# A fused attention and feed-forward kernel: static PSUM tiles in place of pools, two score tiles ahead of the values, and copies issued one step later

## The chip, the core and the metric

The kernel runs on one core of a Trainium2 chip. TensorE (PE) multiplies and writes PSUM, VectorE (DVE) and ScalarE (ACT) read PSUM and work on SBUF, GpSimd (POOL) works on SBUF and issues the loads, SyncE (SP) issues stores and transposing transfers. The metric is the device time of one execution in microseconds (us). Each engine runs its instructions in order; semaphores order the engines among each other.

## What is computed

Attention with a cumulative decay over 8 batches of 8 heads (576 positions, head dimension 64), then a two-layer network over all 4608 positions:

```python
scores = q @ k.T / sqrt(D)
cum = cumsum(log(clip(f, 1e-4, 1)))
scores = where(causal, -1e9, scores + cum[i] - cum[j])
attn = softmax(scores)
x = (attn @ v), heads side by side       # 4608 x 512
h = x @ w_in                             # 512 x 2048
out = (h - tanh(h)) @ w_out              # 2048 x 512
```

Inputs and output are float32; the matmuls run on float16 operands.

## The kernel before

Attention is done in 32 *slots*, one for each batch and each pair of heads. A slot has seven *score tiles* (ti 0 to 6): a score tile is one or two matmuls of L384 (with some small ones for decay and mask in the first slots) into one PSUM bank, an exp by ACT from PSUM to SBUF (L399), and in slots from 5 on a causal mask by POOL (L413). After ti 1 of a slot come the *values* of the slot before: thirty matmuls of L423 into the `av` bank pair, then division by DVE (L429 to L431) to `xn`, then `turn`, which transposes `xn` into the ring `XR` (by PE in batch 0, by transposing DMA later).

The network is done in nine *units* of 512 positions. A unit has sixteen *mlp1 tiles*: four matmuls of L458 into one bank from `m_bank()`, tanh by ACT to `th` (L465), and `gt = mb + th` by DVE (L476; tanh is taken of the negative). Then come fourteen *product* steps (L512), eight matmuls each. They form the second layer by a scheme of seven block products: three running sums X, W and Y in PSUM, each read when a part of it is final. X is copied to SBUF as `part` by ACT (L519) after products 1, 6 and one more, and goes on accumulating in the same bank; `settle` adds a bank to such a part by DVE (L545, L542) or copies it out by ACT (L536), and stores it. For units from 1 on X lies in the bank of `ps_tr`, W and Y come from `m_bank()`.

The order of everything is written out by hand; no scheduler moves it. `first_slot` runs the first five slots by the lists in `FIRST` ("g" is a group of two score tiles, "s" one score tile, "va" and "vb" the values of the two heads, "x" and "y" a turn, "h" an mlp1 tile without its last matmul, "m" one network step). From slot 5 on `att_items` lists a slot's attention work, and the loop at the end deals network steps (`step()`, L587) between it: seven or eight a slot, five in slots 5 to 7, so that 30 steps of a unit take four slots. A score tile and a network step mostly alternate; in a slot with eight steps ti 0 and ti 1 stand together, in one with seven also ti 2 and ti 3. Units 7 and 8 are the tail: no scores are left there.

PSUM has eight banks. Two hold `av`, one is `ps_tr`. The other five change hands at slot 4: up to slot 3 they are one bank for transpositions (`ps_t2`) and two pairs for groups of scores (`ps_two`); from slot 4 on three for `m_bank()` (`ps_m`) and two for single score tiles (`ps_sc`). The pools hand out a new tile at each call, and the framework puts a semaphore wait in front of the first write to it, on the last reader of the tile that had this place before.

In slots 7 and 8, `trans` brings the next batch's Q and K from PSUM to SBUF by ACT ("AA") in place of DVE ("VV") for some calls.

Of the kernel before, what the change touches and what calls it, by code (L numbers as in the profile page):

```python
# [8 lines left out]
FP32 = mybir.dt.float32  # L9
FP16 = mybir.dt.float16  # L10
AF = mybir.ActivationFunctionType
# [12 lines left out]
def kernel(  # L24
# [10 lines left out]
    nc = tc.nc  # L35
    P = 128
# [6 lines left out]
    NPAIR = H // 2  # L43
# [6 lines left out]
    UW = 512  # L50
# [11 lines left out]
    PSUM = bass.MemoryType.PSUM  # L62
    ps_av = ctx.enter_context(tc.tile_pool(name="ps_av", bufs=1, space=PSUM))
    ps_tr = ctx.enter_context(tc.tile_pool(name="ps_tr", bufs=1, space=PSUM))
    POOLS = {}
    turn_of = [0]

    def m_bank():
        return POOLS["m"].tile([P, UW], FP32, tag="m", name="mb")

    win = wpl.tile([P, NCH, DFF], FP16)
    wout = wpl.tile([P, NFT, DM], FP16)
# [7 lines left out]
    qn, kn = ([t[0:S // NT6, :].rearrange("p (h n d) -> p h n d", h=H, n=NT6) for t in raw] for raw in (qraw, kraw))  # L80
# [218 lines left out]

    def t_bank():  # L300
        turn_of[0] += 1
        if "t" in POOLS and turn_of[0] % 2:
            return POOLS["t"].tile([P, UW], FP32, tag="t2", name="t32")
        return ps_tr.tile([P, UW], FP32, tag="tr", name="t32")

    def trans(b, c, src, dst, engs):
# [31 lines left out]
    LAST = 3  # L338
# [18 lines left out]

    def scores(b, c, tis, how):
        n2 = len(tis)
        if "t" in POOLS and tis[0] == LAST:  # L360
            banks = t_bank().rearrange("p (o w) -> p o w", o=1)
        else:
            banks = POOLS["s"].tile([P, 2 if "t" in POOLS else 1, UW], FP32, tag="sc", name="ps")
        if tis[0] == LAST:
            eb = EL[(b * NPAIR + c) % 3].rearrange("p (o w) -> p o w", o=1)
        else:
            g, o = PLACE[tis[0]]
            if b == 0:
                if o == 0:
                    EB[(b, c, g)] = gtp.tile([P, 2, UW], FP16, tag="gt", name="e2")  # L370
                eb = EB[(b, c, g)][:, o:o + n2, :]
            else:
                eb = aex.tile([P, 1, UW], FP16, tag="e", name="e")
        late = []
        for i, ti in enumerate(tis):
            ps, e = banks[:, i, :], eb[:, i, :]
            for a, j, i0, n, col in TILES[ti]:
                h = 2 * c + a
                while late and late[-1][2] is ps:
                    decay(*late.pop(0))  # L380
                edge = min(P, n) if how != "late" and i0 == j * P else 0
                direct = b == 0 and (h == 0 or h == 1 and ti in (4, 5))
                rows = D if direct and h else D + 3
                nc.tensor.matmul(out=ps[:, col:col + n], lhsT=KT[b % 2][0:rows, h, j * P:(j + 1) * P],  # L384
                                 rhs=QT[b % 2][0:rows, h, i0:i0 + n], start=True, stop=not (edge or direct))
                args = (b, h, ps, j, i0, n, col, edge, direct)
                if direct and len(tis) > 1:
                    late.append(args)
                else:
                    decay(*args)  # L390
                for ib in range(j, NJ):
                    w0 = min(ib * P, S - P)
                    if i0 <= ib * P < i0 + n:
                        E[(b, c, a, j, ib)] = e[:, col + w0 - i0:col + w0 - i0 + P]
        for args in late:
            decay(*args)
        lo = min(x[4] for x in TILES[tis[0]])
        hi = max(x[4] + x[3] for x in TILES[tis[0]])
        nc.scalar.activation(out=eb[:, :, lo:hi], in_=banks[:, 0:n2, lo:hi], func=AF.Exp, scale=qscale)  # L399
        if how != "late":  # L400
            return
        ti, e = tis[0], eb[:, 0, :]
        col, cp, step, wd = MASKS[ti]
        dims = [[step, cp, 0]] * (cp > 1)
        if b < FAR:
            dims = dims + [[D, wd // D, D]] * (wd > D) + [[D // 2, 2, 1], [1, D // 2, 2]]
        else:
            dims = dims + [[1, wd, 1]]
        parts = [(0, dims)] if len(dims) < 4 else [(o * step, dims[1:]) for o in range(cp)]
        for o, dims in parts:  # L410
            view = e[:, col + o:col + o + wd]
            view = bass.AP(view.tensor, view.offset, [list(view.ap[0])] + [[x, n] for x, n, _ in dims])
            nc.gpsimd.affine_select(out=view, in_=view, compare_op=ALU.is_ge, fill=0.0,  # L413
                                    base=0, pattern=[[y, n] for _, n, y in dims], channel_multiplier=-1)
# [65 lines left out]
    def sums(u, i, which):  # L480
# [5 lines left out]
        for n in which:  # L486
# [2 lines left out]
            eng = nc.gpsimd if (n < 3 and i < 2 or n == 2 and i == 2) and u > NU - 3 else nc.vector  # L489
            eng.tensor_tensor(out=dst, in0=x, in1=y, op=op)  # L490

    def product(u, n, g):
        t0 = g * P
        chain = (1, 6, 7, 4) if u == 0 else (1, 6, 5, 3)
        where = "X" if n in chain else "W" if n == 2 else "Y"
        last = u == NU - 1 and where == "Y"
        if last:
            where += str(g)
        first = n in (1, 2, 5 if u == 0 else 7)
        if first and (g == 0 or last):  # L500
            M2[(u, where)] = ps_tr.tile([P, DM], FP32, tag="tr", name="px") if where == "X" and u else m_bank()
        ps = M2[(u, where)]
        left = {1: lambda k: GT[(u, k)][:, t0:t0 + P],
                2: lambda k: GT[(u, K2 + k)][:, t0:t0 + P],
                3: lambda k: SUM[(u, k // 2)][:, 2, k % 2, t0:t0 + P],
                4: lambda k: GT[(u, K2 + k)][:, T2 + t0:T2 + t0 + P],
                5: lambda k: SUM[(u, k // 2)][:, 0, k % 2, t0:t0 + P],
                6: lambda k: SUM[(u, k // 2)][:, 1, k % 2, t0:t0 + P],
                7: lambda k: GT[(u, k)][:, T2 + t0:T2 + t0 + P]}[n]
        right = {1: B11, 2: B21, 3: B22, 4: WT4, 5: WT1, 6: WT2, 7: WT3}[n]  # L510
        for k in range(K2):
            nc.tensor.matmul(out=ps[:, g * E2:(g + 1) * E2], lhsT=left(k), rhs=right[:, k, :],  # L512
                             start=(first and (g == 0 or last) and k == 0), stop=(k == K2 - 1), skip_group_check=True)
        if last:
            settle(u, n, ps, g)
        elif g == 1 and n in chain[:3]:
            part = osp.tile([P, DM], FP32, tag="ost", name="part")
            PART[(u, n)] = part
            nc.scalar.activation(out=part, in_=ps, func=AF.Copy)  # L519
            if u == 0 and n == 7:  # L520
                settle(u, 7, M2[(u, "Y")])
        elif g == 1 and not (u == 0 and n == 5):
            settle(u, n, ps)
        for i, w in LATER[min(u, 1)].get((n, g), ()):
            sums(u, i, (w,))
# [59 lines left out]
    STEPS = [0]  # L585

    def step():  # L587
        for fn, *args in mlp[STEPS[0]]:
            fn(*args)
        STEPS[0] += 1  # L590
# [6 lines left out]

    def first_slot(p):
        here = pairs[p]
# [41 lines left out]
    def att_items(p):  # L641
        items = []
        before = pairs[p - 1]
        after = pairs[p + 1] if p + 1 < len(pairs) else None
        for ti in range(len(TILES)):
            if p < len(pairs):
                items.append((lambda ti=ti: scores(*pairs[p], (ti,), "late"), True))
            items += [(load, False) for load in LOADS.get((p, ti), ())]
            if after and after[0] < FAR and ti in TURNED.get(p, (0, 3)):
                dst, src = (KT, kn) if ti == TURNED.get(p, (0, 3))[1] else (QT, qn)  # L650
                items.append((lambda dst=dst, src=src, p=p: trans(*after, src, dst, "AA" if p == 2 * NPAIR or p == 2 * NPAIR - 1 and src is qn else "VV"), True))
            if ti == 1:
                items += [(lambda a=a: values(*before, a), a == 1) for a in range(2)]
                items.append((lambda: turn(*before), True))
        return items

    with tc.tile_pool(name="ps_t2", bufs=1, space=PSUM) as POOLS["t"]:
        with tc.tile_pool(name="ps_two", bufs=2, space=PSUM) as POOLS["s"]:
            for p in range(NPAIR):
                first_slot(p)  # L660
    del POOLS["t"]
    POOLS["m"] = ctx.enter_context(tc.tile_pool(name="ps_m", bufs=3, space=PSUM))
    POOLS["s"] = ctx.enter_context(tc.tile_pool(name="ps_sc", bufs=2, space=PSUM))
    first_slot(NPAIR)
    for p in range(NPAIR + 1, len(pairs) + 1):
        items = att_items(p)
# [38 lines left out]
```

## Time and profile before

| | us |
|---|---|
| median of three runs | 341.51 |
| lowest, highest | 341.25, 343.12 |
| the profiled execution | 342.1 |
| its span, first to last instruction | 340.3 |

TensorE's granted clock was 1.00 over the span. Rows of the timeline give the start, the duration, engine and line, output and inputs, how many instructions were merged, and in brackets how long the engine had been idle before and what it waited for. Rows of the view of waits give total, number and longest. Rows of busy time by stage give the window, its length, and busy time and number of instructions on PE, PE's weight loads, DVE, ACT and POOL, then clock, DMA share and GB/s. Rows of the chain of waits give start, duration and line. The end of a matmul is modelled: a matmul's row overlaps the next one's, so a tile's cost to PE is read from start to start.

### The profile page before, as it was taken

Reading aid. Unit: us, or ns where it says so; the run is one execution under the profiler, and the core shown is the slowest. Engines: PE = TensorE matmul, PEld = TensorE weight load, DVE = VectorE, ACT = ScalarE, POOL = GpSimd, SP = SyncE. Lnnn points to the kernel's source line nnn. Section 1 sums busy time; section 2 is a strip of 40 time slices with the busy share of each in tenths; the row PEclk is TensorE's granted clock in tenths of the full one; section 3 lists DMA queues with packets and bytes.
Section 4 is the critical chain, followed back from the end, with each engine's and each line's share of the span. In section 5 each row is a group of like instructions: output and inputs, shape, how many; then the busy total and the mean of one; then the engine's idle time right before and its main releaser. Section 6 shows DMA issues by size and latency. Waiting matters only on the chain.

```text
span 340.3 us, 8718 instructions
## 1 busy us (share of the span) xinstructions
PE 332.6 (98%) x3307; PEld 233.9 (69%) x3307; DVE 254.6 (75%) x521; ACT 218.2 (64%) x409; POOL 186.8 (55%) x341
## 2 busy tenths in 40 slices
PE   8999999899999999999999999999999999999996
PEld 3585558675687558887785578656877786486485
DVE  6676999769996789478956897489748864873872
ACT  6585888567755886588657865687558843733631
POOL 8988487976887557763777276732322220500510
PEclk9999999999999999999999999999999999999999
DMA  9999999999999959999999999992130013003003
GB/s 94 159 186 178 197 178 135 102 201 154 160 113 161 204 75 91 155 161 140 79 118 171 143 104 111 170 164 57 52 105 12 17 49 110 0 23 104 3 0 125
DMA packets 162776, 38.82 MB, mean 114 GB/s; under 512 B 149122, under 2 KB 162670, under 8 KB 162734
## 3 DMA queue, kind: packets, MB, share of 16 engines
q0 software_dynamic: 109664, 18.36, 83.5%
q1 hardware_dynamic: 53070, 19.90, 32.0%
q8 instruction: 26, 0.43, 0.6%
q14 instruction: 16, 0.13, 0.2%
HBM read 36.85 MB, written 9.44 MB: 136 GB/s over the span
## 4 chain that ended last, share of the span: by engine, by line
PE 92%; DVE 3%; ACT 2%; POOL 1%; issue 1%; ACTq 0%
PE mb L458 36%; PE px L512 16%; PE mb L512 15%; PE ps L384 12%; PE av L423 8%; PE spin L298 2%; PE t L311 1%; ACT e L399 1%; POOL e L413 1%; DVE xn L431 1%; DVE KT L326 1%; DVE QT L326 0%; PE ps L350 0%; PE ps L355 0%; PE ps L352 0%
## 5 line engine op out<-in xcount | busy, mean ns | idle before, releaser
L458 PE MATMUL mb<-XR,win 128*128 128x512 f16 (+4 forms) x704 | 141.1, 340 | 0.0
L399 ACT ACTIVATE e<-ps 128x512 f16<-128x512 f32 (+1 forms) x182 | 109.2, 622 | 24.3 <-PE ps L384 15.3
L413 POOL TENSOR_SCALAR_AFFINE_SELECT e<-e 128x128 f16<-128x128 f16 x176 | 67.1, 388 | 91.8 <-ACT e L399 90.9
L465 ACT ACTIVATE th<-mb 128x512 f32<-128x512 f32 x144 | 86.5, 601 | 48.2 <-PE mb L458 46.0
L476 DVE TENSOR_TENSOR gt<-mb,th 128x512 f16<-128x512 f32 x144 | 97.6, 688 | 23.8 <-ACT th L465 23.4
L458 PEld LDWEIGHTS <-win 128*128 128x128 f16 x704 | 61.7, 97 | 47.7 <-issue 1.5
L384 PE MATMUL ps<-QT,KT 67*128 67x64 f16 (+5 forms) x376 | 73.8, 278 | 1.1 <-ACT e L399 0.4
L512 PEld LDWEIGHTS <-gt 128*128 128x128 f16 x576 | 53.7, 97 | 10.9 <-issue 1.0
L384 PEld LDWEIGHTS <-KT 67*128 67x128 f16 (+1 forms) x384 | 36.2, 98 | 22.7 <-issue 3.1
L512 PEld LDWEIGHTS <-sm 128*128 128x128 f16 x432 | 40.5, 97 | 6.5 <-issue 0.2
L512 PE MATMUL mb<-ws,gt 128*128 128x256 f16 x288 | 36.4, 272 | 0.0
L423 PEld LDWEIGHTS <-e 128*128 128x128 f16 x896 | 32.1, 97 | 5.0 <-POOL e L413 1.3
L423 PE MATMUL av<-vn,e 128*128 128x65 f16 x896 | 33.8, 193 | 1.6 <-POOL e L413 1.1
L519 ACT ACTIVATE part<-px 128x512 f32<-128x512 f32 x24 | 14.3, 597 | 30.1 <-PE px L512 30.1
L512 PE MATMUL px<-ws,sm 128*128 128x256 f16 x256 | 31.6, 272 | 0.0
L545 DVE TENSOR_TENSOR part<-mb,part 128x512 f32<-128x512 f32 x25 | 17.1, 686 | 17.4 <-PE mb L512 9.7
L120 POOL DMA_DIRECT2D vn<-in_v_dram x32 | 28.5, 896 | 2.2 <-issue 1.2
L431 DVE TENSOR_TENSOR xn<-av,rs 128x640 f16<-128x640 f32 x32 | 26.4, 825 | 1.1
L490 POOL TENSOR_TENSOR sm<-gt 128x512 f16<-128x512 f16 x4 | 4.6, 1154 | 33.1 <-DVE gt L476 33.1
L429 DVE TENSOR_SCALAR rs<-av 128x10 f32<-128x10 f32 x32 | 5.2, 161 | 23.4 <-PE av L423 23.1
L101 POOL DMA_DIRECT2D qn<-in_q_dram x25 | 21.7, 868 | 1.1 <-issue 1.0
L101 POOL DMA_DIRECT2D kn<-in_k_dram x25 | 21.6, 864 | 1.2 <-issue 1.1
(91 smaller groups left out, 324.1 us busy)
## 6 DMA issues: line engine op xcount, KB each, us to landing
out_dram<-part SPq DMA_DIRECT2D x24, 256.0 KB
vn<-in_v_dram POOLq DMA_DIRECT2D x32, 128.0 KB, 6.1
qn<-in_q_dram POOLq DMA_DIRECT2D x20, 128.0 KB, 5.0
kn<-in_k_dram POOLq DMA_DIRECT2D x20, 128.0 KB, 4.4
win<-in_moe_w_in_dram POOLq DMA_DIRECT2D x4, 512.0 KB, 8.4
wout<-in_moe_w_out_dram POOLq DMA_DIRECT2D x2, 1024.0 KB, 17.9
out_dram<-ost SPq DMA_DIRECT2D x8, 256.0 KB
qn<-in_q_dram POOLq DMA_DIRECT2D x10, 144.0 KB, 6.7
```

What stands on the lines that cost most here:

```text
L101: nc.gpsimd.dma_start(out=dst[b % 2][0:pn, n, :].rearrange("p (h d) -> p h d", h=H), in_=src[b, :, n * P:n * P + pn, :].rearrange("h p d - ...
L120: nc.gpsimd.dma_start(out=vn[b % 2][:, n, h0:h1, 0:D], in_=v[b, h0:h1, n * P:(n + 1) * P, :].rearrange("h p d -> p h d"))
L384: nc.tensor.matmul(out=ps[:, col:col + n], lhsT=KT[b % 2][0:rows, h, j * P:(j + 1) * P], rhs=QT[b % 2][0:rows, h, i0:i0 + n], start=True, ...
L399: nc.scalar.activation(out=eb[:, :, lo:hi], in_=banks[:, 0:n2, lo:hi], func=AF.Exp, scale=qscale)
L413: nc.gpsimd.affine_select(out=view, in_=view, compare_op=ALU.is_ge, fill=0.0, base=0, pattern=[[y, n] for _, n, y in dims], channel_multip ...
L423: nc.tensor.matmul(out=av[:, a, ib, :], lhsT=E.pop((b, c, a, j, ib)), rhs=vn[b % 2][:, j, 2 * c + a, 0:D + 1], start=(j == 0), stop=(j == ib))
L431: nc.vector.tensor_tensor(out=xn.rearrange("p i (a d) -> p a i d", a=2), in0=av[:, :, :, 0:D], in1=rs.to_broadcast([P, 2, NJ, D]), op=ALU. ...
L458: nc.tensor.matmul(out=hps[:, o:o + n], lhsT=win[:, ci, ft * P:(ft + 1) * P], rhs=XR[:, ci, t:t + n], start=(ci == 0), stop=(ci == NCH - 1))
L465: nc.scalar.activation(out=th, in_=hps, func=AF.Tanh, scale=-1.0)
L476: nc.vector.tensor_tensor(out=to, in0=x, in1=y, op=ALU.add)
L512: nc.tensor.matmul(out=ps[:, g * E2:(g + 1) * E2], lhsT=left(k), rhs=right[:, k, :], start=(first and (g == 0 or last) and k == 0), stop=( ...
L545: nc.vector.tensor_tensor(out=ost, in0=ps, in1=ost, op=ALU.add)
```

## The change

It has four parts.

- The five banks are three tiles that live through the program: TB (a pair), TA (a pair) and TT (one). Up to slot 3 groups of scores alternate between TB and TA, and TT serves transpositions. From slot 4 on score tiles alternate between the halves of TB, and `m_bank()` goes round TT, TA's first half, TA's second half.
- In slot 4 the first two score tiles stand ahead of the values.
- ACT's copy of X to `part` (and in unit 0 the `settle` of product 7 on DVE) isn't issued at once, but kept in a list that is emptied behind the next exp, or at the start of the next network step, whichever comes first.
- In slot 8 the two copies of a transposed Q go from ACT to DVE.

```diff
-    POOLS = {}
+    ps_x = ctx.enter_context(tc.tile_pool(name="ps_x", bufs=1, space=PSUM))
+    TB, TA = (ps_x.tile([P, 2, UW], FP32, tag=f"t{i}", name=f"t{i}") for i in "ba")
+    TT = ps_x.tile([P, UW], FP32, tag="tt", name="tt")
+    MBANKS = [TT, TA[:, 0, :], TA[:, 1, :]]
+    EARLY = [True]
+    COUNT = {"m": 0, "s": 0}
+
+    def turn_about(what):
+        COUNT[what] += 1
+        return COUNT[what] - 1
...
     def m_bank():
-        return POOLS["m"].tile([P, UW], FP32, tag="m", name="mb")
+        return MBANKS[turn_about("m") % 3]
...
     def t_bank():
         turn_of[0] += 1
-        if "t" in POOLS and turn_of[0] % 2:
-            return POOLS["t"].tile([P, UW], FP32, tag="t2", name="t32")
+        if EARLY[0] and turn_of[0] % 2:
+            return TT
         return ps_tr.tile([P, UW], FP32, tag="tr", name="t32")
...
     def scores(b, c, tis, how):
         n2 = len(tis)
-        if "t" in POOLS and tis[0] == LAST:
+        if EARLY[0] and tis[0] == LAST:
             banks = t_bank().rearrange("p (o w) -> p o w", o=1)
         else:
-            banks = POOLS["s"].tile([P, 2 if "t" in POOLS else 1, UW], FP32, tag="sc", name="ps")
+            i = turn_about("s") % 2
+            banks = (TB, TA)[i] if EARLY[0] else TB[:, i:i + 1, :]
...
         nc.scalar.activation(out=eb[:, :, lo:hi], in_=banks[:, 0:n2, lo:hi], func=AF.Exp, scale=qscale)
+        flush()
...
+    PENDING = []
+
+    def flush():
+        while PENDING:
+            PENDING.pop(0)()
...
-            nc.scalar.activation(out=part, in_=ps, func=AF.Copy)
+            PENDING.append(lambda: nc.scalar.activation(out=part, in_=ps, func=AF.Copy))
             if u == 0 and n == 7:
-                settle(u, 7, M2[(u, "Y")])
+                PENDING.append(lambda: settle(u, 7, M2[(u, "Y")]))
...
     def step():
+        flush()
         for fn, *args in mlp[STEPS[0]]:
...
-             ["c", "va", "y", "vb", "s0", "s1", "h0", "h1", "x", "h2", "q1", "s2", "m", "s3", "m", "s4", "k1", "m", "s5", "m", "s6", "m"]]
+             ["c", "s0", "s1", "va", "y", "vb", "h0", "h1", "x", "h2", "q1", "s2", "m", "s3", "m", "s4", "k1", "m", "s5", "m", "s6", "m"]]
...
-                items.append((lambda dst=dst, src=src, p=p: trans(*after, src, dst, "AA" if p == 2 * NPAIR or p == 2 * NPAIR - 1 and src is qn else "VV"), True))
+                items.append((lambda dst=dst, src=src, p=p: trans(*after, src, dst, "AA" if (p, src is qn) in ((2 * NPAIR - 1, True), (2 * NPAIR, False)) else "VV"), True))
...
-    with tc.tile_pool(name="ps_t2", bufs=1, space=PSUM) as POOLS["t"]:
-        with tc.tile_pool(name="ps_two", bufs=2, space=PSUM) as POOLS["s"]:
-            for p in range(NPAIR):
-                first_slot(p)
-    del POOLS["t"]
-    POOLS["m"] = ctx.enter_context(tc.tile_pool(name="ps_m", bufs=3, space=PSUM))
-    POOLS["s"] = ctx.enter_context(tc.tile_pool(name="ps_sc", bufs=2, space=PSUM))
+    for p in range(NPAIR):
+        first_slot(p)
+    EARLY[0] = False
     first_slot(NPAIR)
```

## The prediction

> **What bounds the kernel now.** I read the page's busy times first, then what TensorE waits for, then the costliest groups.
>
> ```profile
> span 340.3 us, 8718 instructions
> PE 332.6 (98%) x3307; PEld 233.9 (69%) x3307; DVE 254.6 (75%) x521; ACT 218.2 (64%) x409; POOL 186.8 (55%) x341
> ...
> L458 PE MATMUL mb<-XR,win 128*128 128x512 f16 (+4 forms) x704 | 141.1, 340 | 0.0
> L399 ACT ACTIVATE e<-ps 128x512 f16<-128x512 f32 (+1 forms) x182 | 109.2, 622 | 24.3 <-PE ps L384 15.3
> ...
> L465 ACT ACTIVATE th<-mb 128x512 f32<-128x512 f32 x144 | 86.5, 601 | 48.2 <-PE mb L458 46.0
> L476 DVE TENSOR_TENSOR gt<-mb,th 128x512 f16<-128x512 f32 x144 | 97.6, 688 | 23.8 <-ACT th L465 23.4
> ```
>
> PE is busy for all but 7.7 us of the span. The first-layer matmuls of L458 never waited (idle 0.0) because three PSUM banks stand between them and their readers; ACT and DVE waited for PE. The view of waits, kept to PE, shows what there is to win in the middle of the span:
>
> ```profile
> PE av L423 <- POOL e L413: 1.1, 2, 0.9
> PE av L423 <- DVE xn L431: 0.5, 1, 0.5
> ```
>
> So at best 1.6 us could come back; all the rest is risk. What matters is whether PE can still run ahead of its readers.
>
> **What the change does to the waits.** I compared the waits in the two built programs. POOL's and SP's instructions stand in the same order in both; no DMA is added or moved. But the wait in front of each write to PSUM is now kept for a whole tile, and the change makes one tile of two banks. Before, every mlp1 tile waits for the `gt` three tiles back, and every score tile for the exp two back. After, with TT, then TA's first half (A0), then TA's second half (A1) in turn: A1 waits for the `gt` of the A0 tile just before it, A0 for the `gt` of A1 two back, TT still three back. Every score tile, in one or the other half of TB, waits for the exp of the score tile just before it. This holds to the last unit.
>
> **The price of one such wait.** The timeline of the tail, where mlp1 runs without scores, gives the chain from a matmul tile to its free bank:
>
> ```profile
> 284.81 14.02 PE L458 MATMUL mb<-XR,win 128*128 128x512 f16 x64
> ...
> 285.87 0.60 ACT L465 ACTIVATE th<-mb 128x512 f32<-128x512 f32 x1 [2.01 <-PE mb L458]
> 286.50 0.69 DVE L476 TENSOR_TENSOR gt<-mb,th 128x512 f16<-128x512 f32 x1 [0.80 <-ACT th L465]
> ```
>
> `th` starts 1.06 us after its tile's first matmul, and `gt` ends at 287.19, 2.38 us after it. How fast PE resumes is read where it does wait:
>
> ```profile
> 25.61 0.82 DVE L431 TENSOR_TENSOR xn<-av,rs 128x640 f16<-128x640 f32 x1
> ...
> 26.50 0.59 PE L423 MATMUL av<-vn,e 128*128 128x65 f16 x14 [0.51 <-DVE xn L431]
> ...
> 31.33 0.60 ACT L399 ACTIVATE e<-ps 128x512 f16<-128x512 f32 x1 [2.02 <-PE ps L355]
> ...
> 31.98 0.38 PE L384 MATMUL ps<-QT,KT 67*128 67x512 f16 x1
> ```
>
> 26.50 less 26.43 is 0.07 us after DVE, 31.98 less 31.93 is 0.05 us after ACT. So a tile that must wait for the one before it starts 2.38 + 0.07 = 2.45 us after that one's start. For scores:
>
> ```profile
> 109.80 0.60 ACT L465 ACTIVATE th<-mb 128x512 f32<-128x512 f32 x1 [2.38 <-PE mb L458]
> ...
> 110.29 0.59 ACT L399 ACTIVATE e<-ps 128x512 f16<-128x512 f32 x1
> ...
> 110.68 0.22 PE L384 MATMUL ps<-QT,KT 67*128 67x64 f16 x2
> ...
> 110.75 1.03 PE L458 MATMUL mb<-XR,win 128*128 128x512 f16 x4
> ...
> 111.38 0.27 ACT L399 ACTIVATE el<-ps 128x128 f16<-128x128 f32 x1
> ...
> 131.80 0.38 PE L384 MATMUL ps<-QT,KT 67*128 67x320 f16 x2
> ...
> 132.02 1.04 PE L512 MATMUL px<-ws,sm 128*128 128x256 f16 x8
> ...
> 132.28 0.60 ACT L399 ACTIVATE e<-ps 128x512 f16<-128x512 f32 x1 [0.50 <-PE ps L384]
> ...
> 132.89 0.38 PE L384 MATMUL ps<-QT,KT 67*128 67x512 f16 x1
> ```
>
> A score tile takes PE 0.22 us (131.80 to 132.02; the narrow tile ti 3 0.07, from 110.68 to 110.75, its exp 0.27), its exp starts 0.48 us after it, and the next score tile can start 0.48 + 0.60 + 0.05 = 1.13 us after its start. Where a `th` or a copy stands first on ACT, exp starts 0.50 behind that one (109.80 to 110.29), and the sum is 0.20 + 0.50 + 0.60 + 0.05 = 1.35. Where a product (0.87 us) lies between two score tiles, as from 131.80 to 132.89, 1.09 passes anyway and next to nothing is lost; where two stand together, 1.13 or 1.35 less 0.22 is: 0.91 or 1.13 us.
>
> **The tail** (units 7 and 8). From the chain of waits and the busy times by stage:
>
> ```profile
> 284.97 13.85 PE mb L458 x64
> ...
> 72.39:91.92 19.53, 19.52 (x174) 10.66 (x171) 17.99 (x35) 14.73 (x29) 14.62 (x29) 1.00 2.41 170
> 108.73:127.37 18.64, 18.61 (x150) 9.76 (x148) 15.35 (x28) 14.83 (x29) 9.92 (x20) 1.00 1.28 141
> ...
> 252.00:271.00 19.00, 18.98 (x217) 13.56 (x215) 15.28 (x29) 14.91 (x30) 4.72 (x14) 1.00 0.12 31
> ```
>
> A tile's own time is 13.85 / 16 = 0.87. The turn begins at A0 in every unit but the first (19 banks are drawn in unit 0, 18 in each later one). A0 at 0, A1 at 2.45, TT behind it at 3.32, the next A0 at 2 x 2.45 = 4.90. Five such turns of three and the sixteenth tile: 25.4 us, against 13.85: 11.5 more, twice: **23.0**.
>
> **mlp1 with scores** (units 1 to 6; the rows above are units 1, 2 and 6). I laid out unit 2 by these numbers in PE's order: t0 ti2 t1 ti3 t2 ti4 t3 ti5 t4 ti6 t5 ti0 ti1 t6 values t7 t8 ti2 ti3 t9 ti4 t10 ti5 t11 ti6 t12 ti0 ti1 t13 values t14 t15, with 0.90 us for values:
>
> ```profile
> 134.37 0.90 PE av L423 x30
> ```
>
> Starts of t0 to t15: 0, 2.45, 3.38, 4.90, 7.35, 8.44, 10.91, 13.36, 14.23, 16.50, 18.95, 20.04, 21.40, 23.85, 25.63, 26.50, and the end at 27.4. t6, t9 and t15 wait for nothing themselves but stand behind score pairs or values; t1, t3, t4, t7, t10, t12 and t13 start exactly when a `gt` frees TA. Against 18.64 that is 8.7 more; against 19.00 in unit 6, 8.4; unit 1, whose three transpositions mostly fit into the idle time, 27.7 against 19.53, 8.2. Six at 8.5: **51**.
>
> **Products** (units 1 to 5). In each, ti 3 comes 0.25 late behind `th` of t15, three pairs of score tiles stand together (0.91, 0.91, and 1.13 where the copy of product 3 is ahead on ACT), and single ones lose about 0.1. The deferred copy adds its own: it now runs behind an exp.
>
> ```profile
> L519 ACT ACTIVATE part<-px 128x512 f32<-128x512 f32 x24 | 14.3, 597 | 30.1 <-PE px L512 30.1
> ```
>
> Behind (1, 1) it ends 0.48 + 0.50 + 0.60 = 1.58 after the score tile's start, and (6, 0), which writes the same bank, would start at 1.32 or so: 0.3 lost. Bounds for the deferral: nothing where no score tile stands between, 0.6 (a whole copy) at each of three copies a unit. 3.6 a unit, five times, and 0.6 in unit 6: **18.7**.
>
> **Unit 0 and slot 4.** s0 and s1 ahead of values cover the 0.51 us wait for `xn`, but s1 must wait for s0's exp, 0.87: a loss of 0.4. In the rest of slot 4 one-matmul tiles and scores alternate, and both waits bite: 0.65 + 0.46 + 0.67 + 0.18, with the 0.4 **2.3**. In slots 5 to 7 two or three score tiles stand together seven times, some with a transposition between, and A1 waits three times: **8.4**. Here X and Y of the products lie in the two halves of TA, so (5, 0) waits for the copy of product 1 (1.4), (4, 0) for copy and settle of 7 (1.05); with three score pairs, 5.5, less the 1.1 that values waited for POOL, whose masks gain time: **4.4**. Together 15. Bounds: 5 (each wait hidden by transpositions and values) to 25 (two more tile waits of 1.5 in each of three slots).
>
> The two copies of slot 8 that move from ACT to DVE (0.45 us each there) fall into time in which DVE waits for `th`; without that cover they would cost 0.9.
>
> **Sum.** 23.0 + 51 + 18.7 + 15 = 107.7 on a span of 340.3: 448. The profiled execution took 342.1, 1.8 more than its span and 0.6 over the median of 341.51, so 449.8 as profiled and **449** as a median.
>
> **The rivals.**
>
> *DVE in the way.* The sum has `gt` start as soon as `th` is there. In unit 2 DVE was busy 15.35 us, 16 x 0.69 = 11.0 of it with `gt`; 4.3 are sums, values' divisions and placings. Against it: while PE waits for a `gt`, DVE has 1.7 us free from M's start to `th`'s end. If half of these 4.3 stood before a gating `gt` in six units, 13 more: 462; if all, 475. Chance 0.13.
>
> *The clock.* The first matmuls of the span, after 1.45 us without work, took 3.59 / 8 = 0.45 us each, the next 1.49 / 7 = 0.21:
>
> ```profile
> 1.45 3.59 PE L298 MATMUL spin<-ones 128*128 128x512 f16 x8 [1.45 <-DVE ones L160]
> 4.41 1.49 PE L298 MATMUL spin<-ones 128*128 128x512 f16 x7
> ```
>
> In the new tail PE idles up to 1.6 us at a time and works 55% of it. If it fell to half rate there, a turn would be 2 x (2.45 + 0.87) = 6.64, 9.6 a unit: 468; in units 1 to 6 too, up to 520. Against it: the 14 matmuls behind the wait of 0.51 us at 26.50 took 0.59 us in all, and the granted clock reads 1.00 in every stage. Chance 0.06. The Trainium skill (TensorE: Matmul & The Clock Gate, "A second HAM failure mode: psum-queue depth-cycling") reports a kernel whose TensorE idles briefly between groups as it cycles through PSUM banks, and whose clock then swings; by it this rival's time would hold.
>
> *Score waits hidden.* If exps ran early enough, or the halves of TB did not hold each other up, products lose nothing, slots 5 to 7 and unit 0 some 10 less, and mlp1 1.7 less a unit: 449 - 18.7 - 10 - 10 = 410. Against it: ACT starts an exp 0.48 us behind its scores even when idle. Chance 0.05.
>
> *Not slower.* If a half of TA could be written while the other is read, every tile wait would be satisfied as before; the one mechanism that would remain is the new order, which hides 0.5 at slot 4 and loses about 1.5 at the deferred copies: 342.5. It decides at the first A1 tile of unit 1: does it start before the `gt` of the A0 tile? The built program speaks against it, the wait stands there. Chance 0.03. The Trainium skill (PSUM — Partial Sum Buffer, "PSUM bank collisions raise a hardware error") asks only that engines be kept apart by bank and quadrant, and these halves are different banks; by that rule the chip would allow this rival's time.
>
> **How the numbers follow.** The forecast as worked out has 0.73; its own range is 432 to 464, from unit 0's bounds (-10, +10) and some 5% on the 93 of the other terms. To 472 most of DVE in the way and the lighter clock case come in. Below 432 lie the last two rivals, above 472 the heavier clock case. A measurement of this kernel can tell about 0.5%, 1.7 us. Faster by more 0.01, within it 0.02, slower 0.97.
>
> **What would show it.** In the tail, starts of mlp1 tiles 2.45, 0.87 and 1.58 us apart in turn, a unit's sixteen tiles in 25.4 us, and L458 waiting for DVE `gt`, 1.58 us in front of A1 and 0.71 in front of A0 in each turn of the tail, tens of us in total on the list of PE's waits, where now there is none. L384 waiting for ACT exp by tens of us. PE busy near 75% of the span with the clock at 1.00. A `gt` that starts later than 0.03 us behind its `th` in front of an A1 tile would be DVE in the way. I am wrong if L458 still waits for nothing.

## The result and the profile after

| | before | after |
|---|---|---|
| median, us | 341.84 | 453.98 |
| lowest, highest | 341.25, 343.12 | 450.32, 455.83 |
| the profiled execution | 342.1 | 450.32 |
| its span | 340.3 | 448.5 |

The ratio is 1.329, with a 95% interval of 1.324 to 1.334: the kernel became a third slower. Ratios here and below leave out executions more than 1.5% above the fastest of the same kernel, so they can differ a little from the ratio of the medians. From the page of the changed kernel, busy times and the costliest groups; line numbers have moved by some ten, L469 is the L458 of before, L394 the L384, L409 the L399, L476 the L465, L487 the L476, L529 the product of L512, L536 the copy to `part` of L519, L562 the `settle` of L545:

```profile
span 448.5 us, 8713 instructions
PE 352.1 (79%) x3307; PEld 236.2 (53%) x3307; DVE 256.5 (57%) x523; ACT 224.4 (50%) x407; POOL 183.4 (41%) x341
...
L469 PE MATMUL ta<-XR,win 128*128 128x512 f16 (+2 forms) x480 | 101.8, 341 | 47.1 <-DVE gt L487 46.2
...
L469 PE MATMUL tt<-XR,win 128*128 128x512 f16 (+4 forms) x224 | 47.5, 340 | 0.0
```

The same 3307 matmuls are done, and DVE, ACT and POOL are busy within 7 us of before. The span grew by 108.2 us, nearly all of it time in which PE stands still. PE's busy time grew by 19.5 us with no more work: it counts the 0.17 us by which a modelled row ends late, once at each of some hundred waits, and 1.7 us of a half-speed clock (last section). That is also why the share reads 79% and not the 75% of the prediction. Read the two rows of L469 together: tiles in `tt` still wait for nothing, tiles in `ta` wait 47.1 us. PE's view of waits, where before there was 1.6 us to be won:

```profile
PE ta L469 <- DVE gt L487: 46.2, 52, 1.4
PE tb L394 <- ACT e L409: 38.4, 45, 1.0
PE spin L307 <- DVE ones L169: 1.5, 1, 1.5
PE ta L529 <- ACT part L536: 1.2, 1, 1.2
PE tb L394 <- ACT el L409: 1.0, 2, 0.7
PE ta L529 <- DVE part L562: 0.8, 1, 0.8
```

The list sums to less than 108 because a matmul's row runs 0.17 us past the moment at which the next could start, so each gap shows shorter than it is: 1.41 for 1.58, 0.55 for 0.72. The tail's timeline shows the turn of three itself:

```profile
370.32 1.03 PE L469 MATMUL ta<-XR,win 128*128 128x512 f16 x4
...
371.38 0.60 ACT L476 ACTIVATE th<-ta 128x512 f32<-128x512 f32 x1 [2.01 <-PE ta L469]
372.01 0.69 DVE L487 TENSOR_TENSOR gt<-ta,th 128x512 f16<-128x512 f32 x1 [0.80 <-ACT th L476]
372.76 1.02 PE L469 MATMUL ta<-XR,win 128*128 128x512 f16 x4 [1.41 <-DVE gt L487]
373.62 1.03 PE L469 MATMUL tt<-XR,win 128*128 128x512 f16 x4
...
375.19 1.02 PE L469 MATMUL ta<-XR,win 128*128 128x512 f16 x4 [0.55 <-DVE gt L487]
```

The second `ta` tile starts 2.44 us after the first, 0.06 us after the first one's `gt` has ended (372.70), though it writes the other bank; `tt` follows 0.86 later, and the next `ta` tile 1.57 after that, 0.05 us behind a `gt`. The turn takes 4.87 us where three tiles took 2.6. By stages, busy times of the changed kernel for mlp1 and products of unit 1, mlp1 of units 2 and 6, and mlp1 of unit 7:

```profile
87.74:115.83 28.09, 20.96 (x168) 10.82 (x166) 18.21 (x37) 15.53 (x29) 14.05 (x28) 1.00 1.12 102
115.83:136.18 20.35, 17.74 (x197) 14.50 (x196) 11.90 (x27) 10.06 (x19) 13.85 (x26) 1.00 1.12 119
136.18:163.76 27.58, 20.29 (x151) 9.97 (x149) 16.21 (x31) 15.49 (x29) 9.11 (x19) 1.00 0.80 81
328.00:355.71 27.71, 20.43 (x214) 13.71 (x212) 15.49 (x28) 15.49 (x29) 4.59 (x14) 1.00 0.08 21
370.32:395.54 25.22, 15.41 (x66) 6.19 (x64) 11.49 (x17) 8.97 (x15) 5.77 (x5) 1.00 0.06 21
```

### The profile page after: what moved, and what is told of

Its sections match the earlier page's. It is cut to its first block, busy times and chain, and to the rows that moved or that the text cites. A ratio compares the mean times of both kernels' runs of the same rounds, so it can differ in the third digit from the quotient of the medians.

```text
span 448.5 us, 8713 instructions
## 1 busy us (share of the span) xinstructions
PE 352.1 (79%) x3307; PEld 236.2 (53%) x3307; DVE 256.5 (57%) x523; ACT 224.4 (50%) x407; POOL 183.4 (41%) x341
## 4 chain that ended last, share of the span: by engine, by line
PE 56%; ACT 20%; DVE 16%; issue 5%; DMA 1%; POOL 0%; ACTq 0%; DVEq 0%
PE ta L469 19%; DVE gt L487 11%; PE px L529 11%; ACT th L476 10%; ACT e L409 8%; PE tt L529 6%; PE tb L394 5%; PE av L434 5%; PE ta L529 4%; PE tt L469 3%; DVE sm L501 1%; ACT part L536 1%; DVE xn L442 1%; PE ta L394 1%; DVE KT L335 1%
## 5 line engine op out<-in xcount | busy, mean ns | idle before, releaser
L409 ACT ACTIVATE e<-tb 128x512 f16<-128x512 f32 (+1 forms) x175 | 106.3, 607 | 65.7 <-PE tb L394 58.4
L469 PE MATMUL ta<-XR,win 128*128 128x512 f16 (+2 forms) x480 | 101.8, 341 | 47.1 <-DVE gt L487 46.2
L487 DVE TENSOR_TENSOR gt<-ta,th 128x512 f16<-128x512 f32 x98 | 67.7, 691 | 88.5 <-ACT th L476 88.2
L469 PEld LDWEIGHTS <-win 128*128 128x128 f16 x704 | 63.2, 97 | 103.1 <-issue 60.3
L476 ACT ACTIVATE th<-ta 128x512 f32<-128x512 f32 x98 | 58.6, 598 | 103.0 <-PE ta L469 103.0
L394 PE MATMUL tb<-QT,KT 67*128 67x64 f16 (+4 forms) x355 | 75.0, 278 | 41.2 <-ACT e L409 38.4
L394 PEld LDWEIGHTS <-KT 67*128 67x128 f16 (+1 forms) x384 | 36.6, 97 | 70.7 <-issue 49.1
L529 PEld LDWEIGHTS <-gt 128*128 128x128 f16 x576 | 53.8, 97 | 10.2 <-issue 0.9
L469 PE MATMUL tt<-XR,win 128*128 128x512 f16 (+4 forms) x224 | 47.5, 340 | 0.0
L529 PEld LDWEIGHTS <-sm 128*128 128x128 f16 x432 | 41.0, 97 | 8.7 <-issue 2.7
L487 DVE TENSOR_TENSOR gt<-tt,th 128x512 f16<-128x512 f32 x46 | 31.7, 690 | 16.8 <-ACT th L476 16.8
L476 ACT ACTIVATE th<-tt 128x512 f32<-128x512 f32 x46 | 27.5, 598 | 17.3 <-PE tt L469 16.4
L529 PE MATMUL px<-ws,sm 128*128 128x256 f16 x256 | 31.5, 272 | 0.7
L529 PE MATMUL tt<-ws,gt 128*128 128x256 f16 x240 | 30.4, 272 | 0.0
L501 POOL TENSOR_TENSOR sm<-gt 128x512 f16<-128x512 f16 x4 | 4.6, 1153 | 48.3 <-DVE gt L487 48.3
L562 DVE TENSOR_TENSOR part<-tt,part 128x512 f32<-128x512 f32 x15 | 10.3, 688 | 22.0 <-PE tt L529 14.3
```

The source lines that it names most:

```text
L469: nc.tensor.matmul(out=hps[:, o:o + n], lhsT=win[:, ci, ft * P:(ft + 1) * P], rhs=XR[:, ci, t:t + n], start=(ci == 0), stop=(ci == NCH - 1))
L476: nc.scalar.activation(out=th, in_=hps, func=AF.Tanh, scale=-1.0)
L487: nc.vector.tensor_tensor(out=to, in0=x, in1=y, op=ALU.add)
L562: nc.vector.tensor_tensor(out=ost, in0=ps, in1=ost, op=ALU.add)
```

## The experiments

The theory: the loss is the waits held per tile, of mlp1 on `gt` and of scores on exp, and nothing else in the change costs or brings more than about a microsecond. The rivals: the other three edits carry part of it; one of the two kinds of wait hides behind the other; tiles that live through the program cost by themselves. Ratios are to the kernel before, measured beside each.

### The static tiles alone, and everything but the static tiles

The first kernel is that of before with the new tiles alone: `m_bank`, `t_bank`, `scores` and the end as in the change, without `PENDING`, with the old list for slot 4 and "AA" as before.

> The kernel before with the static PSUM tiles alone; order of slot 4, copies and transpositions as before. If the waits held per tile carry the loss: 445 to 456 us, with L458-type tiles waiting some 46 us for gt and score tiles some 38 us for exp on the list of TensorE's waits, as in the changed kernel. If the deferred copies or the new order carried a good part of it: under 435.

455.02 us, ratio 1.325 (1.314 to 1.337). Its waits on PE:

```profile
PE ta L468 <- DVE gt L486: 46.2, 53, 1.4
PE tb L394 <- ACT e L409: 40.1, 46, 1.1
```

The second kernel is the changed one with the pools put back (`m_bank`, `t_bank` and `scores` as before too):

```diff
...
-    for p in range(NPAIR):
-        first_slot(p)
-    EARLY[0] = False
+    with tc.tile_pool(name="ps_t2", bufs=1, space=PSUM) as POOLS["t"]:
+        with tc.tile_pool(name="ps_two", bufs=2, space=PSUM) as POOLS["s"]:
+            for p in range(NPAIR):
+                first_slot(p)
+    del POOLS["t"]
+    POOLS["m"] = ctx.enter_context(tc.tile_pool(name="ps_m", bufs=3, space=PSUM))
+    POOLS["s"] = ctx.enter_context(tc.tile_pool(name="ps_sc", bufs=2, space=PSUM))
```

> The changed kernel with the pools of before; new order, deferred copies and moved transposition kept. Waits held per tile: 338 to 344 us, TensorE's waits under 5 us in all. If the other three edits cost by themselves (a deferred copy 0.3 us twice a unit at the least): 343 to 346; if they carried the loss: over 350.

342.56 us, ratio 1.003 (1.0006 to 1.0053). So the static tiles make nearly the whole loss, and the rest of the change costs about 1 us beside pools. The largest part of that stands in the timeline of this second kernel, PE and ACT in unit 0 (L519 is the product here, L526 the copy):

```profile
64.26 1.30 ACT L324 ACTIVATE KT<-t 64x576 f16<-64x576 f16 x2 [0.85 <-PE t L311]
...
65.59 0.60 ACT L399 ACTIVATE e<-ps 128x512 f16<-128x512 f32 x1
66.08 0.59 ACT L526 ACTIVATE part<-mb 128x512 f32<-128x512 f32 x1
66.56 0.60 ACT L399 ACTIVATE e<-ps 128x512 f16<-128x512 f32 x1
66.73 1.03 PE L519 MATMUL mb<-ws,gt 128*128 128x256 f16 x8 [1.19 <-ACT part L526]
```

The deferred copy of product 7 now stands behind a transposition's two copies and an exp on ACT, and (4, 0), which goes on in the same bank, waits 1.19 us for it. Before, the copy ran ahead of all three. The rest of PE's list nearly cancels: 0.4 us more for an exp, 0.4 for a `gt` and 0.3 for KT, against 1.4 less for POOL's masks and `xn`.

### One kind of wait at a time

The third kernel is that of before with only the two late score banks as halves of one tile, the fourth with only two of the three mlp banks as halves of one.

```diff
-            banks = POOLS["s"].tile([P, 2 if "t" in POOLS else 1, UW], FP32, tag="sc", name="ps")
+            if "t" in POOLS:
+                banks = POOLS["s"].tile([P, 2, UW], FP32, tag="sc", name="ps")
+            else:
+                banks = TB[0][:, half[0]:half[0] + 1, :]
+                half[0] = 1 - half[0]
...
-    POOLS["s"] = ctx.enter_context(tc.tile_pool(name="ps_sc", bufs=2, space=PSUM))
+    POOLS["s"] = ctx.enter_context(tc.tile_pool(name="ps_sc", bufs=1, space=PSUM))
+    TB[0] = POOLS["s"].tile([P, 2, UW], FP32, tag="sc", name="tb")
```

> The kernel before, only the two late score banks made halves of one tile; mlp1 keeps three tiles. By the terms of the sum: pairs of score tiles lose 0.91 or 1.13, and each single one between mlp1 tiles 1.35 less 1.09, some 33 us in units 1 to 6, 18 in the products, 9 in unit 0: 401 us (390 to 412), with TensorE waiting only for exp. If score waits hide behind other work: 342 to 350.

394.45 us, ratio 1.154 (1.147 to 1.161). PE waits 38.9 us for exp and not at all for `gt`. The score waits don't hide; the time lies in the range, 6.5 us under its middle. The timeline shows why (L463 is mlp1, L389 scores, L404 exp):

```profile
127.12 1.03 PE L463 MATMUL mb<-XR,win 128*128 128x512 f16 x4
128.24 0.22 PE L389 MATMUL tb<-QT,KT 67*128 67x64 f16 x2
...
129.38 1.03 PE L463 MATMUL mb<-XR,win 128*128 128x512 f16 x4
...
130.49 0.38 PE L389 MATMUL tb<-QT,KT 67*128 67x448 f16 x2
...
130.71 1.03 PE L463 MATMUL mb<-XR,win 128*128 128x512 f16 x4
...
130.97 0.60 ACT L404 ACTIVATE e<-tb 128x512 f16<-128x512 f32 x1
...
131.62 0.38 PE L389 MATMUL tb<-QT,KT 67*128 67x320 f16 x2
...
132.91 0.38 PE L389 MATMUL tb<-QT,KT 67*128 67x512 f16 x1
134.03 0.38 PE L389 MATMUL tb<-QT,KT 67*128 67x448 f16 x2 [0.75 <-ACT e L404]
```

With 0.86 us for the mlp1 tile, the score tile at 128.24 is 0.26 late as expected and the one at 130.49 0.25, but the one at 131.62, behind a late one, only 0.05; and the pair is 1.12 apart (0.90 lost) rather than 1.35. A score tile that starts late lets `th` get ahead on ACT, so its own exp finds ACT free and starts 0.48 us behind it (130.97), and the next score tile is hardly held. mlp1 of this unit ends with 3.9 us lost (126.04 to 148.59, 22.55 against 18.64), where 5.5 were reckoned.

```diff
+    MBANKS, taken = [], [0]
+
     def m_bank():
-        return POOLS["m"].tile([P, UW], FP32, tag="m", name="mb")
+        taken[0] += 1
+        return MBANKS[(taken[0] - 1) % 3]
...
-    POOLS["m"] = ctx.enter_context(tc.tile_pool(name="ps_m", bufs=3, space=PSUM))
+    POOLS["m"] = ctx.enter_context(tc.tile_pool(name="ps_m", bufs=1, space=PSUM))
+    TT = POOLS["m"].tile([P, UW], FP32, tag="tt", name="tt")
+    TA = POOLS["m"].tile([P, 2, UW], FP32, tag="ta", name="ta")
+    MBANKS.extend([TT, TA[:, 0, :], TA[:, 1, :]])
```

> The kernel before, only two of the three mlp banks made halves of one tile; score tiles keep two. By the terms of the sum: 11.5 us in each unit of the tail, turns of 4.90 us without score pairs in units 1 to 6 (6.7 a unit more), some 5 in unit 0: 409 us (400 to 418), with the tail's tiles 2.45, 0.87 and 1.58 us apart. If one wait a turn were enough to hide the other: under 390.

414.53 us, ratio 1.213 (1.207 to 1.220); PE waits 60.6 us for `gt`, in 65 places; that is 5.5 us over the middle of the range. The tail of its trace has the tiles 2.43 to 2.44, 0.86 and 1.57 us apart, as forecast. Score waits and `gt` waits alone add 53 and 73 us, 126 together, and both at once 112. The lists say which shrinks: beside each other, exp still costs PE 38.4 us but `gt` only 46.2 instead of 60.6, so part of the wait for `gt` runs under that for exp.

### One tile a bank

Now the cure that the theory names: the same static banks, each as a tile of its own. A group of two score tiles in the first slots then needs an exp for each bank.

```diff
-    TB, TA = (ps_x.tile([P, 2, UW], FP32, tag=f"t{i}", name=f"t{i}") for i in "ba")
+    TB, TA = ([ps_x.tile([P, UW], FP32, tag=f"t{i}{o}", name=f"t{i}{o}") for o in range(2)] for i in "ba")
...
-    MBANKS = [TT, TA[:, 0, :], TA[:, 1, :]]
+    MBANKS = [TT, TA[0], TA[1]]
...
-        nc.scalar.activation(out=eb[:, :, lo:hi], in_=banks[:, 0:n2, lo:hi], func=AF.Exp, scale=qscale)
+        for i in range(n2):
+            nc.scalar.activation(out=eb[:, i, lo:hi], in_=banks[i][:, lo:hi], func=AF.Exp, scale=qscale)
```

> The changed kernel with each of the five banks a static tile of its own; the exp of a group of two score tiles in the first slots becomes two exps, one for each bank. Waits held per tile: 338 to 345 us, waits at the distances of before. If tiles that live through the program cost by themselves, whatever their size: over 350.

341.43 us, ratio 1.0014 (0.9993 to 1.0035): a tile that lives through the program costs nothing that can be told from noise; a tile of two banks whose halves are meant to be independent costs a third of the kernel. The wait for the deferred copy is still there, 1.2 us, so the deferral was taken back too:

```diff
-            PENDING.append(lambda: nc.scalar.activation(out=part, in_=ps, func=AF.Copy))
+            nc.scalar.activation(out=part, in_=ps, func=AF.Copy)
             if u == 0 and n == 7:
-                PENDING.append(lambda: settle(u, 7, M2[(u, "Y")]))
+                settle(u, 7, M2[(u, "Y")])
```

> One static tile a bank with the new order of slot 4, but the copies of X issued at once as before. If the deferral is what costs the 1.2 us that TensorE waits for a copy in unit 0, that wait is gone and the time is 339.8 to 340.8 us, 0.5 to 1.5 below the kernel before (0.5 of waiting for xn and 1.1 for POOL gone). If the deferral is free: 341 to 342, as with it.

340.20 us, ratio 0.9979 (0.9965 to 0.9994): with one tile a bank, the new order of slot 4, the moved transposition and copies at once it is 0.2% faster than the kernel before, and has the lowest median of all here. The list of what PE waits for at other engines, headed by its start, has nothing left from the middle of the span above 0.2 us but 0.6 for a `gt`:

```profile
PE spin L307 <- DVE ones L169: 1.4, 1, 1.4
PE ta L530 <- DVE gt L502: 0.6, 1, 0.6
PE tb L359 <- DVE cc L200: 0.2, 1, 0.2
```

### The clock

The changed kernel's four runs took 450.32, 452.69, 455.27 and 455.83 us at mean granted clocks of 0.995, 0.988, 0.985 and 0.981. Whether idle time pulls the clock down was tried by filling it. First the changed kernel again, then with matmuls that nobody reads, into the bank of `ps_tr`, which is idle during mlp1 from unit 2 on.

> The changed kernel again, for its clock: 450 to 456 us with a mean granted clock of 0.98 to 0.995, longer where the clock is lower. If the spread were something else: times that do not follow the clock.

455.11 us, ratio 1.322 (1.316 to 1.329). The six runs took 449.07 us at a clock of 0.999, 450.11 at 0.996, 454.12 and 456.10 at 0.981, 456.68 at 0.977 and 459.34 at 0.969. The range was too narrow at both ends, but the time follows the clock.

```diff
+        fill = {0: 4, 1: 0, 2: 2 * (u > 6)}[COUNT["m"] % 3] * (u > 1)
+        if fill:
+            t32 = ps_tr.tile([P, UW], FP32, tag="tr", name="fill")
+            for _ in range(fill):
+                nc.tensor.matmul(out=t32, lhsT=ones16[:, 0:P], rhs=ones16[:, 0:UW])
```

> The changed kernel with matmuls into an idle PSUM bank (4 ahead of each A1 tile in units 2 to 8, 2 ahead of each A0 tile in the tail), nobody reads them. If TensorE's idle time lets its clock fall: a clock nearer to 1.00 in each run and 448 to 452 us with less spread. If the clock falls for another reason: the same clocks and times as the changed kernel, 450 to 456. If the fill stands in the way: over 456 at a full clock.

454.27 us, ratio 1.334 (1.329 to 1.340). Three of five runs, of 453.68 to 454.27 us, were at 1.000, one at 0.996 (455.38), one at 0.985 (458.60). The clock was steadier, but the fill itself cost some 4.6 us against the 449.07 of an unfilled run at 0.999; none of the three forecasts holds as it stands. Then the fill from unit 0 on, with four matmuls between score tiles that stand together there:

> The changed kernel with idle time filled from unit 0 on: 4 matmuls into an idle bank ahead of each A1 tile, 2 ahead of each A0 tile in the tail, and 4 between score tiles that stand together in unit 0. If idle time lets the clock fall: 0.995 to 1.00 in every run and a spread under 3 us, at 453 to 460 us since the fill overshoots in places. If the clock falls for another reason: clocks down to 0.97 in some runs, as in the changed kernel.

473.38 us, ratio 1.387 (1.383 to 1.392), at clocks of 0.986 to 0.996: far above the range. Here the fill takes turns in `ps_tr` with the transpositions and waits for their copies, 10.3 us in all, so it made new gaps, and the clock fell all the same. The traces lean towards idle time: in the two filled kernels every fall of the clock ahead of the last microsecond stands in unit 0 or 1 (one and four of them), while in four traces without fill (the changed kernel twice, the first and the fourth) eight stand in units 2 to 8. With one trace for each filled kernel this is not shown, and these runs don't tell idle time from another cause.

## Why the prediction was right, and where it was not

**The time.** 449 was forecast, 453.98 measured, in the range of 432 to 472. The difference is mostly the clock: 450.32 was the profiled execution at 0.995, and the one run at 0.999 took 449.07. The sum had assumed 1.00. (Two sums are a little off: five times 3.6 and 0.6 are 18.6 and not 18.7, and the bounds named give 434 and not 432 at the low end.)

**The price of a wait.** 2.45 us from a tile's start to the one that waits for it: 2.44 measured. Turns of 4.90 in the tail: 4.87; sixteen tiles in 25.4: 25.2.

**The stages.** mlp1 of unit 2 was laid out to end at 27.4: 27.58. Its first thirteen starts lie within 0.06 us of the layout, the last three 0.21 to 0.23 behind it. The step comes at t13, and DVE makes it:

```profile
157.54 1.02 PE L469 MATMUL ta<-XR,win 128*128 128x512 f16 x4
...
158.60 0.60 ACT L476 ACTIVATE th<-ta 128x512 f32<-128x512 f32 x1 [0.20 <-PE ta L469]
...
159.18 0.42 DVE L501 TENSOR_TENSOR sm<-sm,gt 128x512 f16<-128x512 f16 x1
159.53 0.68 DVE L487 TENSOR_TENSOR gt<-ta,th 128x512 f16<-128x512 f32 x1
...
160.26 1.02 PE L469 MATMUL ta<-XR,win 128*128 128x512 f16 x4
```

t12's `th` starts 1.06 us behind t12, as in the tail, and ends at 159.20; but its `gt` starts 0.33 behind that, since two sums of L501 stand in front of it on DVE, and t13 starts 0.05 behind the `gt`. Unit 1 had 27.7 forecast and took 28.09, unit 6 took 27.71. Products of units 1 to 5 were to lose 3.6 each; unit 1's took 20.35 us from 115.83, against 16.81 before (91.92 to 108.73): 3.54. Unit 2's lost 3.16 (163.76 to 184.11, against 127.37 to 144.56). From start to start, units 1 to 5 grew by 12.1 to 12.3 us each, where 8.5 and 3.6 make 12.1; the tail grew by 22.7 against 23.0. Unit 0 and everything ahead of it, forecast at 15, is read from the start of unit 1: 72.39 before, 87.74 after, 15.35. Here some luck comes in: the stretch of half-speed clock at 48.5 lies in it and takes up to 1.7 us, so the waits themselves made nearer 14.

**The mechanism** is shown, not only fitted: static tiles alone bring the loss, the rest of the change without them does not, and the same banks as single tiles undo it.

**Where it was off.** The term for unit 0's products has the right sizes and half of the cause. From start to start, (5, 0) loses 1.39 us (1.4 forecast) and (4, 0) 0.99 (1.05 forecast), and (4, 0) does wait for the `settle` of product 7 in TA's other half:

```profile
79.83 0.59 ACT L536 ACTIVATE part<-ta 128x512 f32<-128x512 f32 x1
...
80.45 0.69 DVE L562 TENSOR_TENSOR part<-ta,part 128x512 f32<-128x512 f32 x1 [1.97 <-ACT part L536]
...
81.19 1.03 PE L529 MATMUL ta<-ws,gt 128*128 128x256 f16 x8 [0.83 <-DVE part L562]
```

But the term put both waits down to the halves of TA alone, and 2.0 of these 2.4 us need the deferral. With static tiles and copies at once, (5, 0) loses 0.38 and (4, 0) nothing; with the deferral and pools, or one tile a bank, (4, 0) still waits 1.2 us, for the copy in its own bank. In units 1 to 6 the deferred copy makes (6, 0) 0.1 to 0.3 late, as bounded, but it costs nothing there that the traces show: with one tile a bank, the kernels with and without deferral are 0.85 us apart at (6, 0) of unit 1 and 0.83 at that of unit 6. The price of "not slower", 342.5, had put the deferral's loss in those later units; the kernel with pools measured 342.56, so the number held by luck and its reason did not.

**The rivals.** DVE in the way came, but small: by the prediction's own sign, `gt` starts more than 0.03 us behind its `th` in front of an A1 tile once in each of units 2 to 6 (0.32 to 0.33 us, as at t12 above) and twice in unit 1 (0.14 and 0.50), at most some 2 us against the 13 to 26 priced for these units. In unit 0 it comes three times (0.23 to 0.31). In the tail `gt` starts 0.03 behind its `th` (371.98 to 372.01). Score waits hidden: refuted by the third kernel. Not slower: refuted by the first `ta` tiles of unit 1, 2.44 us apart (87.74 and 90.18). The clock came in part, in single stretches and not for whole stages. In the trace of the changed kernel shown above the tail stood at 1.00, but when that kernel was run again each of the tail's two units had one such stretch, and sixteen tiles took 26.2 us instead of 25.2: 1.0 a unit against the 9.6 priced.

## What to carry to other kernels

A tile is the unit in which the framework here keeps its waits: two banks that are to be written and read independently have to be two tiles, however convenient one name for both is, and the waits of the built program show this before anything runs. On a kernel bound by TensorE, price a lost bank by the chain from a matmul tile through its readers to the bank's next use (here 2.45 us against 0.87), and lay it out over one unit in program order. Moving a reader of PSUM behind other work on its engine is free only where it still ends before TensorE goes on in that bank; here it made TensorE wait 1.2 us where two copies of a transposition came between.

## What the runs showed of the hardware that was not expected

TensorE's granted clock fell to half for single stretches, without any long pause ahead of them. In the profiled execution of the changed kernel, busy times by stage (the clock is the third number from the end):

```profile
44.00:48.00 4.00, 2.93 (x19) 1.52 (x19) 1.49 (x3) 2.33 (x5) 2.38 (x7) 1.00 1.48 189
48.00:50.00 2.00, 1.36 (x5) 0.58 (x5) 1.51 (x3) 1.19 (x3) 1.09 (x3) 0.63 1.29 193
50.00:52.00 2.00, 2.00 (x27) 1.45 (x26) 0.40 (x1) 0.60 (x1) 1.11 (x2) 0.52 1.65 188
52.00:54.00 2.00, 1.59 (x17) 0.83 (x15) 1.51 (x4) 0.59 (x2) 0.00 (x0) 1.00 2.22 159
```

0.37 and 0.48 of two windows of 2 us are lost, 1.7 us of clock, as in 3.4 us at half rate; in that stretch a tile of four matmuls has a row of 1.90 us instead of 1.03. Ahead of it PE was busy 73% of 4 us. In this trace the tail, with gaps of 1.6 us and PE busy 61%, stayed at 1.00. In the trace of the same kernel run again it did not:

```profile
394.00:396.00 2.00, 1.02 (x4) 0.38 (x4) 1.37 (x4) 1.04 (x2) 0.23 (x1) 1.00 0.00 0
396.00:398.00 2.00, 1.27 (x4) 0.51 (x4) 0.68 (x1) 0.00 (x0) 0.93 (x1) 0.71 0.00 0
398.00:400.00 2.00, 2.00 (x6) 0.65 (x5) 0.69 (x1) 0.60 (x1) 0.00 (x0) 0.50 0.00 0
400.00:402.00 2.00, 2.00 (x15) 1.34 (x14) 0.86 (x2) 1.20 (x2) 0.00 (x0) 0.94 0.04 8
```

Again 1.7 us of clock are lost (0.58, 1.00 and 0.12). The same size comes out of such windows at every fall ahead of the last microsecond, in all six traces whose clock fell: 1.7 us, and once twice that. Two of these falls stand in the tail of the first kernel, one in that of the fourth. The spread between runs fits this: the profiled run of the changed kernel at 450.32 us has one such stretch, the one at 456.68 us has six. The Trainium skill (TensorE: Matmul & The Clock Gate, "What's actually happening") has the clock judged over windows of about 3.4 us, and the length of these stretches agrees; it has the clock fall after a window of idling, and no such window stands ahead of them: the longest pause of PE in the 5 us ahead of any of these falls is 2.1 us. Its other case, brief idling between groups of matmuls ("A second HAM failure mode: psum-queue depth-cycling"), is nearer to what the traces show. Why the clock falls in some of these places and not in others stays open.
